# One planned issue order for everything ahead of the query phase of a gated mix of an S4 convolution and Hedgehog linear attention

## The chip, the core and the metric

The kernel runs on one core of a Trainium2 chip. Its engines are PE (matmul), DVE (vector), ACT (activations and casts), POOL and SP (which issues most DMAs). Each engine works through its own list of instructions in order, and waits where an instruction's inputs or its output buffer are not ready. The metric is the time of one execution on the device in microseconds (us); smaller is better.

## What is computed

```python
x = A_u                                            # 1 x 2048 x 512, bf16
g = sigmoid((x * gate_w).sum(-1, keepdims=True))
return g * A(x) + (1 - g) * B(x)

def A(u):      # S4: a kernel K per channel from 128 complex modes, then an FFT convolution of length 2*L
    dt = exp(log_dt)[:, None]
    P = exp((dt * (A_re + 1j*A_im))[:, :, None] * arange(L))
    K = einsum("dn,dnl,dn->dl", C, P, dt * B).real
    return irfft(rfft(u, 2*L) * rfft(K, 2*L))[:L] + u * Dskip

def B(x):      # linear attention, 32 heads of 16, feature map from two softmaxes
    q, k, v = split(x @ wqkv)
    phi(t) = concat(softmax(t @ w_phi), softmax(-(t @ w_phi)))
    kv = einsum("bhsf,bhsd->bhfd", phi(k), v);  z = phi(k).sum(s)
    return ((phi(q) @ kv) / (phi(q) @ z + 1e-6)) @ wo
```

## The kernel before

The program has these stages, in the order of the code in `full_kernel`:

- *Tables* (`build_fft_consts`): sine and cosine tables W1, TB, TI, TJ for an FFT that is done as matmuls. Each comes from an iota (POOL), two DVE instructions and one sine (ACT).
- *Rates* (`compute_rates`): the modes' rates as bf16 pairs, sent through DRAM (`pz`) into `stat`.
- *Polar form* (`compute_polar`): the modes' amplitudes and phases as tables Ctab and Dtab. A long chain between DVE and ACT: products, logarithms, exponentials, an arctangent, then four rounds (`trig4`) of fill, reduction, absolute value, two sines and table products.
- *Data turn* (`turn_x`): x (tile UD) is transposed on PE into xT; eight evictions from PSUM.
- *Projections* (`fold_projection`, twice): w_phi is folded into the key and query weights, Wkp and Wqp.
- *Spectrum* (`u_path`): the FFT of x in two halves; each half is eight psA tiles (evicted into XAu), then eight psB tiles (evicted into XU).
- *Gates* (`gates`): the gate g, and its logarithmic form zrow.
- *Key steps* (`key_step`, eight): pk and vp matmuls (projections of keys and values), exponentials Ek (ACT), their sums Zk (a DVE reduction), reciprocals through Ln and Exp (ACT), vr (DVE scaling of the values), and kvp (PE accumulates all steps in one PSUM bank). The first block's query exponentials Eq and the first decay tables (E, cs) are put between steps 4 and 6.
- *Fold* (`fold_kv`): kvp becomes the weights Mw. Its first instruction is zj, its first ACT instruction the cast KVT.
- *Query phase*: four blocks of 512 rows, with the first kernel generators (`kgen`).
- *Convolution* (`convolve`): the rest of the kernel spectrum, the product and the inverse transform.

Up to the query phase the order on each engine is what the tile framework's scheduler makes of this code. The convolution is issued in another way: `Plan` holds pieces of work, each with an engine, a cost in us, dependencies and the rings of buffers that it takes and drops. `Plan.run` lists the pieces by a greedy rule, the piece that can start first, and of those the one with the longest chain behind it (`prio`), and issues them in that order under `manual_schedule`. `late` is the part of a transfer's cost in which SP is already free.

An activation needs its table set on ACT: TRIG has the sine and arctangent, LN_EXP the logarithm and exponential. Changing the set is an ACT_TABLE_LOAD. Ahead of the query phase there are six: TRIG for the tables, LN_EXP for the rates, TRIG for the polar form's second part, LN_EXP for gates and keys, then TRIG and LN_EXP around the first cosines and sines. Evictions go to ACT and DVE in a fixed pattern (`Evict`, "aav": two of three to ACT).

PSUM has two rings of two double banks ahead of the key steps (tags pb and p0). From then on p0's place holds psA: three single banks (bk) and the accumulator kvp.

Of the kernel before, what the change touches and what calls it, by code (L numbers as in the profile page):

```python
# [83 lines left out]
class Tables:  # L84
# [5 lines left out]
    def begin(self, name):  # L90
        p = self.nc.scalar.preload_act_table_set(name)  # L91
        if self.plain:
            return
        order_after(self.tc, p, self.cur)
        self.head, self.cur = p, [p]

    def __call__(self, **kw):
        i = self.nc.scalar.activation(**kw)  # L98
        if self.plain:
            return i  # L100
        order_after(self.tc, i, self.head)
        self.cur.append(i)
        return i
# [12 lines left out]
class Plan:  # L116
# [4 lines left out]
    def __init__(self, rings):  # L121
        self.k, self.nodes = rings, []

    def add(self, eng, cost, fn, deps=(), take=(), drop=(), late=0.0):
        n = Bag()
        n.eng, n.cost, n.fn, n.take, n.drop, n.late = eng, cost, fn, list(take), list(drop), late
        n.deps = [d for d in deps if d is not None]
        n.users, n.t, n.i = [], None, len(self.nodes)
        for d in n.deps:
            d.users.append(n)  # L130
        self.nodes.append(n)
        return n

    def run(self):

        for r, k in self.k.items():
            if r == "ps":
                continue
# [7 lines left out]
        for n in reversed(self.nodes):  # L146
            n.prio = n.cost + n.late + max([u.prio + self.LAT * (u.eng != n.eng) for u in n.users], default=0.0)
# [5 lines left out]
        while left:  # L153
            best = None
            for n in left:
                if any(d.t is None for d in n.deps):
                    continue
                t = free.get(n.eng, 0.0)
                for d in n.deps:
                    t = max(t, d.end + (self.LAT if d.eng != n.eng else 0.0))  # L160
                ok = True
                for r in n.take:
                    if r != "ps":
# [10 lines left out]
                if best is None or key < best[0]:  # L174
                    best = (key, n)
            assert best is not None, "no piece can start"
            (t, _, _), n = best
            n.t, n.end = t, t + n.cost
            free[n.eng] = n.end - (n.late if n.eng == "SP" else 0.0)
            if "ps" in n.take:  # L180
                n.ps = taken["ps"]
                taken["ps"] += 1
            if "ps" in n.drop:
                given["ps"][[d for d in n.deps if "ps" in d.take][0].ps] = n.end
# [361 lines left out]
def attention_consts(nc, wp, icol, ident, gw, Dcol_b, wc):  # L546
    at = Bag()
# [201 lines left out]

def convolve(tc, nc, g):  # L750

    fc, act, XU = g.fc, g.act, g.XU
    P = Plan({"ps": 4, "E": 4, "cs": 4, "A": 2, "R": 2, "KD": 1, "XA": 2, "XK": 2, "tt": 2, "Z": 1, "Zr": 2, "XUs": 1, "bS": 2})
# [8 lines left out]

    def tables(h, prev):

        T = Bag()
        T.E, T.cs, T.nE, T.nc = [None] * 2, [None] * 2, [], []
        for i in range(2):
            G = 2 * h + i
            for b2 in range(2):
                box = Bag()  # L770

                def pe(i=i, G=G, b2=b2, box=box):
                    if b2 == 0:
                        T.E[i] = g.epool.tile([128, 32, 64], BF16, name="E", bufs=4)
                    box.ps = psum([128, 16, 64], "args")
                    for j in range(2):
                        d0 = 16 * b2 + 8 * j
                        nc.tensor.matmul(box.ps[:, 8 * j:8 * j + 8, :], lhsT=g.stat[0:64, G, :], rhs=g.selE[0:64, d0:d0 + 8, :],  # L778
                                         start=True, stop=True, tile_position=(0, 0))

                def ex(i=i, b2=b2, box=box):
                    act(out=T.E[i][:, 16 * b2:16 * b2 + 16, :], in_=box.ps[:], func=ACT.Exp)
                    box.ps = None
                a = P.add("PE", 0.75, pe, [T.first] if b2 else [], take=["ps"] + (["E"] if b2 == 0 else []))
                T.first = a
                T.nE.append(P.add("ACT", 1.03, ex, [a] + prev, drop=["ps"]))
        b = P.add("ACT", 1.28, lambda: act.begin(TRIG), T.nE)
        for i in range(2):
            G = 2 * h + i
            box = Bag()  # L790

            def pe(i=i, G=G, box=box):
                T.cs[i] = g.epool.tile([128, 2, 32, 32], BF16, name="cs", bufs=4)
                box.ps = psum([128, 32, 32], "args")
                for j in range(2):
                    nc.tensor.matmul(box.ps[:, 16 * j:16 * j + 16, :], lhsT=g.stat[64:128, G, :], rhs=g.selE[64:128, 16 * j:16 * j + 16, 32:64],
                                     start=True, stop=True, tile_position=(64, 0))

            def sc(i=i, box=box):
                act(out=T.cs[i][:, 0], in_=box.ps[:], func=ACT.Sin, scale=TWO_PI, bias=HALF_PI)  # L800
                act(out=T.cs[i][:, 1], in_=box.ps[:], func=ACT.Sin, scale=TWO_PI)
                box.ps = None
            a = P.add("PE", 0.75, pe, [T.nE[2 * i]], take=["ps", "cs"])
            T.nc.append(P.add("ACT", 2.06, sc, [a, b], drop=["ps"]))
        T.end = P.add("ACT", 1.28, lambda: act.begin(LN_EXP), T.nc)
        return T
# [252 lines left out]
    T = {}  # L1059
# [10 lines left out]
    for h in range(2, 8):  # L1070
        if h + 1 < 8:
            T[h + 1] = tables(h + 1, prev)
# [17 lines left out]
def full_kernel(tc, A_u, A_A_re, A_A_im, A_B_re, A_B_im, A_C_re, A_C_im, A_log_dt, A_Dskip,  # L1090
# [7 lines left out]
    with ExitStack() as ctx:  # L1098
# [13 lines left out]
        kpool = pool(ck, "kpool")  # L1112
        cu = ExitStack()
        ps0 = pool(cu, "ps0", 2, space=PSUM)
        ring = PsumRing((psP, "pb"), (ps0, "p0"))
        up = pool(cu, "up", side="right")
        xau = pool(cu, "xau", side="right")
        cp = ExitStack()
        tp = pool(cp, "ctmp", side="right")

        UD = up.tile([128, 64, 128], BF16, name="UD")
        for dj in range(4):
            nc.sync.dma_start(out=UD[32 * dj:32 * dj + 32, :, :], in_=x2d[:, 128 * dj:128 * dj + 128].rearrange("(q t) d -> q t d", t=64))
        rawd = {}
        ldc = up.tile([128, 4], BF16, name="ldc")
        ld_b = up.tile([128, 512], BF16, name="ld")
        gw = aq.tile([128, 4], BF16, name="gw")
        Dcol_b = aq.tile([128, 4], BF16, name="Dcol_b")
        wc = up.tile([128, 4, 16], BF16, name="wc")
        with nc.allow_non_contiguous_dma(reason="small"):  # L1130
            for k, src in (("Are", A_A_re), ("Aim", A_A_im), ("Cre", A_C_re), ("Bre", A_B_re), ("Cim", A_C_im), ("Bim", A_B_im)):
                rawd[k] = up.tile([128, 4, 128], BF16, name=k)
                nc.scalar.dma_start(out=rawd[k][:], in_=src.rearrange("(g p) n -> p g n", p=128))
                if k == "Aim":
                    nc.sync.dma_start(out=ldc[:], in_=A_log_dt.rearrange("(g p) -> p g", p=128))
                    nc.sync.dma_start(out=ld_b[:], in_=A_log_dt.partition_broadcast(128))
            nc.sync.dma_start(out=wc[:], in_=B_w_phi.rearrange("(m h) e f -> (h e) m f", h=8))
            nc.sync.dma_start(out=gw[:], in_=gate_w.rearrange("(kt p) -> p kt", p=128))
# [174 lines left out]
```

## Time and profile before

| | |
|---|---|
| median of 3 runs | 377.31 us (377.28 to 377.91) |
| the profiled execution | 376.3 us, its span 374.5 us |
| mean granted TensorE clock in it | 0.852 |
| busy time | DVE 281.4, PE 266.0, ACT 254.8, POOL 8.6 us |
| instructions | 10448 |

Times below are those of the profiled execution, from the span's start, unless the text says otherwise. A row of the timeline has the start, the busy time, engine, line, operation, output<-inputs, size and count; in square brackets stands the idle time ahead of it and what ended it. A row of the groups has the busy time and the mean of one in ns, and behind the second bar the idle time ahead of them. A matmul's busy time contains its latency, so a busy PE is not PE at its peak.

### The profile page before, as it was taken

Reading aid. Unit: us, or ns where it says so; the run is one execution under the profiler, and the core shown is the slowest. Engines: PE = TensorE matmul, PEld = TensorE weight load, DVE = VectorE, ACT = ScalarE, POOL = GpSimd, SP = SyncE. Lnnn points to the kernel's source line nnn. Section 1 sums busy time; section 2 is a strip of 40 time slices with the busy share of each in tenths; the row PEclk is TensorE's granted clock in tenths of the full one; section 3 lists DMA queues with packets and bytes.
Section 4 is the critical chain, followed back from the end, with each engine's and each line's share of the span. In section 5 each row is a group of like instructions: output and inputs, shape, how many; then the busy total and the mean of one; then the engine's idle time right before and its main releaser. Section 6 shows DMA issues by size and latency. Waiting matters only on the chain. (4 is left out here: it accounts for less than half of the span.)

```text
span 374.5 us, 10448 instructions
## 1 busy us (share of the span) xinstructions
PE 266.0 (71%) x4632; PEld 156.6 (42%) x4632; DVE 281.4 (75%) x481; ACT 254.8 (68%) x329; POOL 8.6 (2%) x21
## 2 busy tenths in 40 slices
PE   1225465858997769889998799766778558669662
PEld 0115365755343323334454355333334324437561
DVE  6979778886587537779994545999999997879122
ACT  1668979885744872688647852797799975895520
POOL 4400000000000000000000000000000000000000
PEclk9999996667899966999999999958589856685967
DMA  9994000000000000000000010553957782875311
GB/s 153 161 242 107 0 0 3 2 2 2 0 2 3 2 0 2 2 3 30 28 30 30 8 51 30 137 118 103 162 77 125 158 168 63 147 152 100 61 32 32
DMA packets 77948, 23.62 MB, mean 63 GB/s; under 512 B 72656, under 2 KB 75856, under 8 KB 77904
## 3 DMA queue, kind: packets, MB, share of 16 engines
q1 hardware_dynamic: 73680, 22.05, 29.6%
q10 hardware_dynamic: 4224, 0.92, 1.8%
q8 instruction: 36, 0.59, 0.7%
q14 instruction: 8, 0.07, 0.1%
HBM read 10.90 MB, written 7.86 MB: 50 GB/s over the span
## 5 line engine op out<-in xcount | busy, mean ns | idle before, releaser
L98 ACT ACTIVATE E<-args 128x1024 bf16<-128x1024 f32 x32 | 31.9, 1039 | 4.9 <-PE args L395 4.5
L742 PE MATMUL bps<-Mw,Eq 128*128 128x512 bf16 x128 | 30.4, 380 | 2.5 <-DVE Eq L738 2.3
L645 DVE TENSOR_REDUCE Zk<-Ek 128x64 f32<-128x1024 bf16 x16 | 19.2, 1214 | 17.1 <-ACT Ek L98 17.1
L98 ACT ACTIVATE cs<-args 128x1024 bf16<-128x1024 f32 x32 | 30.9, 1047 | 0.0
L91 ACT ACT_TABLE_LOAD x20 | 25.7, 1283 | 5.4 <-issue 5.1
L738 DVE TENSOR_TENSOR Eq<-Eq,aexp 128x512 bf16<-128x512 bf16 x32 | 20.5, 681 | 11.3 <-PE aexp L735 11.2
L98 ACT ACTIVATE Ek<-pk 128x512 bf16<-128x512 f32 x32 | 17.4, 602 | 13.5 <-PE pk L642 13.5
L450 PE MATMUL kps<-R,A 128*32 128x64 bf16 x1024 | 21.3, 235 | 4.8 <-DVE R L844 4.1
L450 PEld LDWEIGHTS <-A 128*32 128x32 bf16 x1024 | 18.6, 152 | 13.4 <-issue 10.5
L1213 ACT CAST bs<-bps 128x512 bf16<-128x512 f32 x16 | 9.4, 586 | 21.5 <-PE bps L745 17.0
L657 DVE TENSOR_TENSOR vr<-vp,vr 128x512 bf16<-128x512 f32 x32 | 19.9, 682 | 5.3 <-ACT vr L98 4.6
L932 ACT CAST XK<-psB 128x1024 bf16<-128x1024 f32 x16 | 15.9, 1029 | 9.8 <-PE psB L924 8.3
L959 PE MATMUL psz<-t,TI 128*128 128x512 bf16 x48 | 17.0, 477 | 7.3 <-DVE t L939 3.0
L642 PE MATMUL pk<-Wkp,xT 128*128 128x512 bf16 x64 | 20.6, 437 | 1.8 <-ACT Ek L98 1.8
L655 PE MATMUL vp<-Wv,xT 128*128 128x512 bf16 x64 | 19.1, 425 | 2.9 <-ACT Ek L98 2.9
L476 PE MATMUL psB<-XAu,TB 64*128 64x128 bf16 x256 | 12.6, 280 | 11.1 <-ACT XAu L70 4.4
L98 ACT ACTIVATE Eq<-pq 128x512 bf16<-128x512 f32 x32 | 16.5, 612 | 4.2 <-PE pq L699 4.0
L591 PE MATMUL xps<-ident,UD 128*128 128x128 bf16 x64 | 7.5, 311 | 15.7 <-ACT bim L305 9.2
L778 PE MATMUL args<-selE,stat 64*128 64x512 bf16 x40 | 14.6, 476 | 5.4 <-ACT cs L98 2.8
L742 PEld LDWEIGHTS <-Eq 128*128 128x128 bf16 x128 | 11.3, 98 | 16.3 <-DVE Eq L738 4.3
L924 PE MATMUL psB<-XA,TB 64*128 64x64 bf16 (+1 forms) x640 | 12.0, 192 | 7.4 <-issue 1.9
L830 DVE TENSOR_TENSOR A<-A,Atmp 128x1024 bf16<-128x1024 bf16 x24 | 16.6, 692 | 0.8
(228 smaller groups left out, 624.7 us busy)
## 6 DMA issues: line engine op xcount, KB each, us to landing
XUs<-XU SPq DMA_DIRECT2D x6, 512.0 KB, 6.0
Zd<-Zr SPq DMA_DIRECT2D x12, 256.0 KB, 2.2
ZT<-Zd SPq DMA_DIRECT2D x24, 128.0 KB, 3.9
UD<-in_A_u_dram SPq DMA_DIRECT2D x4, 512.0 KB, 11.3
bSd<-bs SPq DMA_DIRECT2D x16, 128.0 KB, 1.7
out_dram<-bS SPq DMA_DIRECT2D x30, 64.0 KB, 2.6
bS<-bSd SPq DMA_DIRECT2D x3, 512.0 KB, 6.1
wqk<-in_B_wqkv_dram SPq DMA_DIRECT2D x1, 1024.0 KB, 5.8
```

The lines of the kernel that those rows point to most:

```text
L91: p = self.nc.scalar.preload_act_table_set(name)
L98: i = self.nc.scalar.activation(**kw)
L450: nc.tensor.matmul(kps[32 * dj:32 * dj + 32, g4, e, :], lhsT=A[:, ri, :, :, d].rearrange("p a b -> p (a b)"), rhs=R[:, ri, d, :], start=(r ...
L642: nc.tensor.matmul(pk[:], lhsT=xT[:, kt, ss], rhs=Wkp[:, kt, :], start=(kt == 0), stop=(kt == 3))
L645: nc.vector.tensor_reduce(out=Zk[:, u, :, :], in_=Ek[:, u, :, :].rearrange("p g (h f) -> p g h f", f=16), axis=mybir.AxisListType.X, op=AL ...
L655: nc.tensor.matmul(vp[:], lhsT=xT[:, kt, ss], rhs=Wv[:, kt, :], start=(kt == 0), stop=(kt == 3))
L657: nc.vector.tensor_tensor(out=vr[:, u, sg, :, 0:32].rearrange("p m (h e) -> p m h e", e=16), in0=vp[:].rearrange("p (m h e) -> p m h e", m ...
L738: nc.vector.tensor_tensor(out=e, in0=e, in1=ps[:], op=ALU.mult)
L742: nc.tensor.matmul(ps[:], lhsT=Eq[:, m, sg, 128 * i:128 * i + 128], rhs=Mw[:, 4 * sg + m, :], start=(k == 0), stop=False, skip_group_check ...
L830: nc.vector.tensor_tensor(out=c.A[:, o], in0=c.A[:, o], in1=tmp[:], op=op)
L932: nc.scalar.copy(out=box.XK[:].rearrange("p s (c e x) -> p (s c) e x", e=2, x=16), in_=box.ps[:].rearrange("p e s (c x) -> p (s c) e x", x ...
L959: nc.tensor.matmul(box.ps[:, 4 * hb:4 * hb + 4, :], lhsT=fc.TI[:, k].rearrange("p a b -> p (a b)"), rhs=box.t[k][:, rt:rt + 4, :], start=( ...
```

## The change

The stages from the tables to the last key step, with the first Eq block and the first tables E and cs, become pieces of one `Plan` (`prepare` and `keys_and_spectrum`), which is issued by hand order, as the convolution already is. The arithmetic stays as it was. What else changes:

- A piece can name keys that it reads and writes (`rw`), from which its dependencies follow. Several PSUM rings can be given out in the order of the plan (`dyn`).
- An eviction can go to ACT or DVE; the plan takes the engine on which it ends first, at costs of 1.1 and 1.3.
- Temporary tiles of the tables and of the polar form get fixed places (`tgv`, `pt`, `pb`, names in the rows below) instead of a ring of nine.
- The transfers start in another order: SP loads log_dt ahead of the four UD loads, and ACT loads its first table set ahead of issuing the six parameter loads.
- The key steps' order allows two steps at a time (Ek, Zk and vr have two buffers, as before).
- `prio` is now `cost` plus the longest chain behind, without adding `late` a second time. This reorders the convolution too.

In the core of the diff, `box`, eviction and load functions are left out:

```diff
-    def add(self, eng, cost, fn, deps=(), take=(), drop=(), late=0.0):
+    def add(self, eng, cost, fn, deps=(), take=(), drop=(), late=0.0, rw=("", "")):
...
+        for k in rw[0].split() + rw[1].split():
+            wr, rd = self.keys.setdefault(k, (None, []))
+            n.deps += ([wr] if wr is not None else []) + (rd if k in rw[1].split() else [])
...
-            n.prio = n.cost + n.late + max([u.prio + self.LAT * (u.eng != n.eng) for u in n.users], default=0.0)
+            n.prio = n.cost + max([u.prio + self.LAT * (u.eng != n.eng) for u in n.users], default=0.0)
...
+def prepare(P, tc, nc, g, evict, psum0):
...
+    t1 = S(1.3, lambda: act.begin(TRIG), w="act")
...
+    S(2.6, params, w="raw0", deps=[t1])
+    P.add("SP", 4.0, lambda: g.load_ld(), late=3.0, rw=("", "ldc ldb"))
+    P.add("SP", 8.0, lambda: None, late=7.9, rw=("raw0", "raw"))
+    for dj in range(4):
+        P.add("SP", 4.0, lambda dj=dj: g.load_ud(dj), rw=("", f"ud{dj}"))
+    P.add("SP", 4.0, lambda: g.load_w(), late=2.0, rw=("", "wsm wqk"))
...
+def keys_and_spectrum(tc, nc, g):
...
+    P = Plan({"XAu": 1, "Ek": 2, "Zk": 2, "vr": 2, "E": 4, "cs": 4}, {"ps": 2, "bk": 3, "p0": 2})
...
+        n.p = P.add([("ACT", 1.1), ("DVE", 1.3)], 1.2, f, deps, drop=[ring])
+        return n.p
+    polar, xt, kp, at_n = prepare(P, tc, nc, g, evict, psum0)
+    lnexp = P.add("ACT", 1.3, lambda: act.begin(LN_EXP), [polar])
...
+            a = P.add("PE", 1.3, pa, [a] if g4 else last, take=[ring] + (["XAu"] if g4 == 0 else []), rw=("ud0 ud1 ud2 ud3 W1", ""))
+            en.append(evict(ea, [a], ring))
...
+            a = P.add("PE", 1.4, pb, en + [a], take=[ring], rw=("TB0 TB1 TB2", ""), drop=(["XAu"] if r0 == 28 else []))
...
+    a = P.add("PE", 4.0, ga, xt + [at_n], take=["ps"])
...
+    a = P.add("PE", 2.0, gd, [b, sp], take=["ps"])
+    P.add("DVE", 0.6, ge, [a], drop=["ps"])
...
+            a = P.add("PE", 1.2, pk, [a] if u else [sp, lnexp] + xt + kp, take=["bk"] + ([] if u else ["Ek", "Zk", "vr"]))
+            x = P.add("ACT", 1.22, ex, [a] + ([x] if u else []), drop=["bk"])
+            red.append(P.add("DVE", 1.21, rd, [x] + red))
...
+        l = P.add("ACT", 0.6, ln, red, drop=["Zk"])
...
+            a = P.add("PE", 1.2, pv, [a], take=["bk"], rw=("wqk", ""))
+            c = P.add("DVE", 1.36, sc, [a, l], drop=["bk"])
+            kv = [P.add("PE", 0.9, kn, [c] + kv, drop=(["Ek", "vr"] if u else []))]
...
+        a = P.add("PE", 1.2, pq, [sh, sp] + ([a] if m else []), take=["bk"])
+        b = P.add("ACT", 1.22, qe, [a], drop=["bk"])
+    sl = P.add("DVE", 3.0, lambda: g.selectors(), [sh, sp, g.n_stat])
+    T = plan_tables(P, nc, g, psum, 0, [n for n in P.nodes if n.eng == "ACT"], [sl])
+    with tc.manual_schedule():
+        act.plain = True
+        P.run()
+        act.plain = False
+    return Q.e, (T.E, T.cs)
```

Three places show how instructions move. The first is on ACT, around its second table load (LN_EXP, ahead of the rates). `tj`, `TI`, `TB` and `w` are parts of the FFT tables. Before:

```order
L98 ACTIVATE w_162<-tg_v,mpi 128x32 x2
L98 ACTIVATE TB<-tg_v,mpi 128x32x64 x2
L98 ACTIVATE TI<-tg_v,mpi 128x64 x2
L98 ACTIVATE tj<-tg_v,mpi 128x1024 x2
L91 ACT_TABLE_LOAD
L98 ACTIVATE dtc<-ldc 128x4
L98 ACTIVATE dt<-ld 128x512
```

and after:

```order
L99 ACTIVATE TB<-tgv_155,mpi 128x32x64
L99 ACTIVATE tj<-tgv_154,mpi 128x1024
L99 ACTIVATE tj<-tgv_155,mpi 128x1024
L1101 CAST XAu<-psA 128x256x4
L91 ACT_TABLE_LOAD
L99 ACTIVATE dtc<-ldc 128x4
L922 COPY pt_261<-psri 128x512
```

A cast of the spectrum's first half, which needs UD, now stands ahead of the load and so ahead of dtc, the first instruction of the rates.

The second place is on ACT around its fourth table load (LN_EXP for the keys). `trg` is a sine of the polar form. Before:

```order
L98 ACTIVATE trg<-big_n 128x1024
L70 CAST XU<-psB 128x32x32 x2
L91 ACT_TABLE_LOAD
L70 CAST XU<-psB 128x32x32 x4
L70 CAST wT_1013<-wtp 128x1024
L70 CAST Wqp<-wps 128x1024
L98 ACTIVATE E<-args 128x1024
L98 ACTIVATE gz<-gz 128x16
L98 ACTIVATE E<-args 128x1024
L98 ACTIVATE Ek<-pk 128x512 x5
```

and after:

```order
L99 ACTIVATE trg<-pb_266 128x1024
L1101 CAST xT<-xps 128x8x4x32 x2
L91 ACT_TABLE_LOAD
L1101 CAST XAu<-psA 128x256x4
L99 ACTIVATE Ek<-pk 128x512 x8
L99 ACTIVATE Zk<-Zk 128x128
L99 ACTIVATE vr<-Zk 128x64x2
L1101 CAST XU<-psB 128x32x32
L99 ACTIVATE Ek<-pk 128x512 x6
```

The key steps come right behind the last XAu cast, and the second half's XU casts, the query projection (wT, Wqp), gate (gz) and tables (E) stand among or behind the key steps.

The third place is on DVE at the start of the key steps. Before:

```order
L259 TENSOR_TENSOR selE<-m_1167,b_1171 128x2048
L68 CAST Wqp<-wps 128x1024
L620 TENSOR_SCALAR gz<-gps 128x16
L631 TENSOR_SCALAR zrow<-zps 128x512
L622 TENSOR_SCALAR gz<-gz 128x16
L623 RECIPROCAL gT<-gz 128x16
L645 TENSOR_REDUCE Zk<-Ek 128x64 x3
L657 TENSOR_TENSOR vr<-vp,vr 128x16x32 x4
L645 TENSOR_REDUCE Zk<-Ek 128x64
```

and after:

```order
L924 TENSOR_TENSOR Dtab<-Dtab,trg 128x4x256 x3
L1099 CAST XAu<-psA 128x256x4 x2
L1258 TENSOR_REDUCE Zk<-Ek 128x64 x4
L1282 TENSOR_TENSOR vr<-vp,vr 128x16x32 x8
L1258 TENSOR_REDUCE Zk<-Ek 128x64 x3
L1099 CAST XU<-psB 128x32x32
L1258 TENSOR_REDUCE Zk<-Ek 128x64
```

The reductions and scalings of two steps stand together, four and eight, and selectors, gate and zrow have left the place ahead of them.

More of the change, by code (lines that the diff above doesn't have):

```diff
@@ L761, in convolve @@
     rkn, xan = [0], [0]
[L763 to L806, printed above, removed]
     def kgen(h, T, XA, new):
@@ L1112, in full_kernel @@
         kpool = pool(ck, "kpool")
+        cz = ExitStack()
         cu = ExitStack()
[L1114 to L1117, printed above, removed]
         cp = ExitStack()
[L1119 to L1123, printed above, removed]
@@ L1130, in full_kernel @@
[L1130 to L1138, printed above, removed]
-            nc.sync.dma_start(out=Dcol_b[:], in_=A_Dskip.rearrange("(kt p) -> p kt", p=128))
@@ new lines, in shift_tmp, with free_tmp, shift_psum @@
+        def shift_tmp():
+            cp.close()
+            g.ctmp = None
+            g.ptmp = pool(cp, "ptmp", side="right")
+        def free_tmp():
+            cp.close()
+            g.kwk = pool(ck, "kwk", 2)
+            g.wo = g.kwk.tile([128, 4, 512], BF16, name="wo_sb", bufs=1)
+            nc.sync.dma_start(out=g.wo[:], in_=B_wo.rearrange("(kt p) c -> p kt c", p=128))
+        def shift_psum():
+            cz.close()
+            g.psA = pool(ca, "psA", 3, space=PSUM)
+            g.kvp = g.psA.tile([128, 8, 34], F32, name="kvp", tag="acc", bufs=1)
```

643 lines of the change are left out of this document (568 added, 75 removed).

## The prediction

> **What bounds the kernel now.** I read the page's busy line first, then the busy time by stages, then the chain, then the timeline at the seams between stages.
>
> ```profile
> PE 266.0 (71%) x4632; PEld 156.6 (42%) x4632; DVE 281.4 (75%) x481; ACT 254.8 (68%) x329; POOL 8.6 (2%) x21
> ```
>
> No engine is full over the whole span, so the question goes to the stages. The columns are the stretch, then busy us of PE, PEld, DVE, ACT and POOL, the granted TensorE clock, the DMA share and GB/s.
>
> ```profile
> 20.00:43.00 23.00, 9.49 (x80) 8.40 (x79) 19.36 (x39) 18.79 (x29) 0.00 (x0) 1.00 0.48 138
> 43.00:77.00 34.00, 22.13 (x272) 19.89 (x272) 28.41 (x45) 27.89 (x30) 0.18 (x1) 0.78 0.00 1
> 77.00:96.00 19.00, 15.50 (x249) 10.92 (x250) 12.46 (x18) 13.85 (x16) 0.00 (x0) 0.68 0.01 2
> 96.00:129.00 33.00, 28.41 (x360) 12.24 (x359) 22.09 (x27) 19.83 (x41) 0.00 (x0) 1.00 0.01 2
> 129.00:147.00 18.00, 13.22 (x156) 4.56 (x156) 10.32 (x14) 11.05 (x18) 0.00 (x0) 0.63 0.00 1
> 147.00:156.60 9.60, 8.35 (x156) 3.69 (x155) 6.23 (x9) 4.24 (x9) 0.00 (x0) 0.98 0.01 2
> 156.60:234.00 77.40, 70.00 (x781) 36.26 (x780) 56.21 (x108) 51.29 (x80) 0.00 (x0) 1.00 0.08 25
> 234.00:346.00 112.00, 80.62 (x1765) 45.47 (x1766) 103.41 (x167) 92.29 (x96) 0.00 (x0) 0.74 0.64 126
> ```
>
> From 43 to 96 ACT and DVE share the polar form and the evictions. From 96 to 156.6 the key steps run: PE is at 50.0 us of 60.6, DVE at 38.6, ACT at 35.1. The first stretch is limited by ACT and DVE, the second by PE and by the round trip between engines, and they stand one behind the other. The query phase (156.6 to 234, PE 90%) and the convolution (DVE 92%) follow and do the same work after the change. The change touches what lies before 156.6, plus the order of the convolution. The seams:
>
> ```profile
> 19.77 0.11 PEld L591 LDWEIGHTS <-UD 128*128 128x128 bf16 x1 [5.53 <-issue]
> 20.72 1.28 ACT L91 ACT_TABLE_LOAD   x1
> 42.91 0.63 ACT L98 ACTIVATE cbi<-cbi 128x512 f32<-128x512 f32 x1
> 81.91 1.28 ACT L91 ACT_TABLE_LOAD   x1
> 95.92 2.20 ACT L98 ACTIVATE Ek<-pk 128x512 bf16<-128x512 f32 x4 [0.58 <-PE pk L642]
> 156.58 0.17 DVE L672 TENSOR_TENSOR zj<-kvp,mask 128x16 f32<-128x16 f32 x1 [0.65 <-PE kvp L663]
> 159.26 1.01 ACT L686 CAST KVT<-ktp 128x1024 bf16<-128x1024 f32 x1
> ```
>
> Here 19.77 is when the matmul side first gets UD, 42.91 is the arctangent (the last step of the polar chain before its trig part), 95.92 the first key exponential, 156.58 the start of the fold. Each term below is a shift of one of these.
>
> **The change, part by part.** The amounts of work stay: PE has the same count of matmuls, ACT the same table loads. Only places move.
>
> *Front, to the arctangent.* SP issues the small log_dt loads ahead of the four UD loads.
>
> ```profile
> 0.73 11.81 SPq L1123 DMA_DIRECT2D UD<-in_A_u_dram  x4
> 12.59 3.22 SPq L1135 DMA_DIRECT2D ldc<-in_A_log_dt_dram  x1
> ```
>
> UD then starts 1 to 4 us later (two short issues, or the whole 3.22 and more), and lands at about 21 to 24. In the new order ACT has one XAu cast, which needs UD, ahead of its second table load: the load moves from 20.72 to about 23 to 25, and the rate and polar chain with it. Against that, ACT evicts less between that load and the arctangent: before it has four xT casts there, now two XAu casts, worth 2 x 1.0 us (DVE has four casts there instead of three). ACT's first table load goes ahead of its six parameter loads; the parameters start 1.28 us later and are needed only behind the second load, so that is hidden, as long as UD, not they, lands last. I take 0 for the arctangent, bounds -1 and +3.
>
> *From the arctangent to the first key step.* This is the main term. Before, 53.0 us lie between 42.91 and 95.92; in them stand the rest of the polar form, both halves of the spectrum, both projections, gates, selectors and two tables. In the new order the key steps' first exponentials come right behind ACT's fourth table load (back to LN_EXP) and one XAu cast. What stands before them on ACT from the arctangent on: 20 casts, 12 polar activations, the arctangent and one load. The eight casts of the spectrum's second half, the second projection, selectors, gates and tables have gone behind. Their prices:
>
> ```profile
> L70 ACT CAST XAu<-psA 128x1024 bf16<-128x1024 f32 x11 | 10.6, 1021 | 2.3 <-PE psA L463 2.2
> L98 ACT ACTIVATE trg<-big_a 128x1024 bf16<-128x1024 f32 x4 | 4.2, 1044 | 0.0
> L98 ACT ACTIVATE Ek<-pk 128x512 bf16<-128x512 f32 x32 | 17.4, 602 | 13.5 <-PE pk L642 13.5
> L645 DVE TENSOR_REDUCE Zk<-Ek 128x64 f32<-128x1024 bf16 x16 | 19.2, 1214 | 17.1 <-ACT Ek L98 17.1
> L657 DVE TENSOR_TENSOR vr<-vp,vr 128x512 bf16<-128x512 f32 x32 | 19.9, 682 | 5.3 <-ACT vr L98 4.6 <-PE vp L655 0.7
> ```
>
> Busy per cast is 10.6 / 11 = 0.96 us (the mean of 1.02 overlaps its neighbour). So 20 x 0.96 + 12 x 1.04 + 0.63 + 1.28 = 33.6 us without a wait. DVE's list over the same stretch comes to about the same: nine casts, the four fills with their reductions, and the table products. ACT was busy 82% of 43 to 77; I take 92%, between that and full, because two kinds of work can now fill each other's waits: 36.5 us, to 79.4, and about 0.5 for the last pk. First key exponential at 79.9 instead of 95.9: **-16.0**. Bounds: no waits, -19; the old 82%, 83.9 + 0.5, -11.5.
>
> *The key steps.* They take 60.7 us now (95.92 to 156.58). The order now does them two at a time: four reductions, then eight scalings on DVE (4 x 1.2 + 8 x 0.62 = 9.8 us), and PE loads vp for both before kvp. Four such pairs are 39 us of DVE. Into the gaps go what was moved behind: eight spectrum casts (7 on ACT, 1 on DVE), four projection casts, selectors 2.7, and the tables.
>
> The price of that is on PE. Its work here at full clock:
>
> ```profile
> 96.83 1.89 PE L655 MATMUL vp<-Wv,xT 128*128 128x512 bf16 x8
> 132.07 1.89 PE L655 MATMUL vp<-Wv,xT 128*128 128x512 bf16 x4
> L476 PE MATMUL psB<-XAu,TB 64*128 64x128 bf16 x128 | 6.0, 277 | 4.0 <-ACT big_n L360 3.4 <-ACT XU L70 0.7
> L618 PE MATMUL gps<-gw,xT 128*128 128x1 bf16 x64 | 1.8, 165 | 0.0
> L627 PE MATMUL zps<-xT,gwr 128*32 128x512 bf16 x16 | 1.9, 628 | 0.0
> ```
>
> Eight matmuls at clock 1.00 cost what four cost in the slow stretch. Counting 129 to 147 at 0.63, PE's 50.0 us are 45 at full clock. The change brings psB 6.0, the second projection about 2.3, gps 1.8, zps 1.9: 12 more, so 57. PE's best share over a long stretch is 70.0 of 77.4, 0.90: 57 / 0.90 = 63.3 us. DVE gives a like figure: 39 + 5.7 for the moved work + about 2.5 of restart after each of three pairs + 6 at the end, where vp waits for the tables' exponentials and the last kvp stand behind zps, which needs a bank that the sines give back: 59. I take 63.5: **+2.8**. Bounds 57 and, with the clock as in 129 to 147, 57 / 0.63 = 90.
>
> The clock decides here: stretches with PE at 86 to 90% show 0.98 to 1.00, those at 65 to 82% show 0.63 to 0.78. The new stretch would have 90%. The Trainium skill ("TensorE: Matmul & The Clock Gate", Part 1) says that the clock is halved by default and that about 3.4 us of sustained matmuls release it; these rows agree. By that rule alone the sum would take the 59 us of the DVE count rather than 63.5.
>
> *Fold to query phase.* ACT has a table load and six Eq exponentials ahead of KVT, whose input is ready 2.7 us after the fold starts (159.26 - 156.58). 1.28 + 6 x 0.54 = 4.5, partly during the last kvp: **+1.5**, bounds 0 and +3.
>
> *The convolution's order.* The planner no longer adds a transfer's late part twice when it ranks pieces, so the rows from 234 on stand differently. At the end:
>
> ```profile
> 346.43 1.31 PE psz L993 x66
> 349.31 0.99 PE psz L993 x38
> 350.30 0.98 PE psA L874 x8
> 351.71 0.62 PE psy L1035 x69
> 359.93 4.29 PE psz L993 x151
> ```
>
> psA stood behind both psz groups and psB behind psy; now psA follows the first psz group, and psB precedes psy. That is worth up to 3 us of the last chain. In the middle DVE has 112.0 - 103.4 = 8.6 us of idle, which another order may halve or double, and nothing here shows which: **-2**, bounds -6 and +6.
>
> Sum: 0 - 16.0 + 2.8 + 1.5 - 2 = -13.7. The profiled execution took 376.3 (span 374.5 and 1.8 around it), so 362.6; the median of the runs, 377.3, is 1.0 above it. I say 363.
>
> **Rivals.** *Fuller overlap.* ACT and DVE run 43 to 79 without waits (-19), PE keeps clock 1.00 and the key steps take 59 (-1.7), the convolution gives 4: about 352 to 354. For it: the query phase reaches 90% on PE. Against: the order's engines are strict queues, and its prices for PE (1.2 for a pk that takes 1.03) shift the real waits.
>
> *The waits move.* The two-at-a-time order waits on banks: vp 4 of a pair cannot start until DVE frees one of three. With the old 82% (-11.5), key steps of 68 (+7.3) and the convolution at 0: 376.3 - 11.5 + 7.3 + 1.5, 373.6; by half of that, 369. For it: ACT idles 13.5 before Ek on pk, and DVE 17.1 before Zk, in the group rows above.
>
> *The clock stays low in the key steps: slower.* PE then carries 57 us of work at about 0.63, as from 129 to 147: 90 us, +29.8 instead of +2.8: 376.3 + 13.3, about 390. It decides where the key steps take 60.7 + 16.0 - 1.5 + 2 = 77 us, a mean clock of 0.74. For it: 43 to 77 and 129 to 147 had PE gaps at every bank change, and the new order puts such changes into the key steps. Against: PE had these at 96 to 129 too and kept 1.00. The Trainium skill ("TensorE: Matmul & The Clock Gate", A second HAM failure mode) describes just that: cycling through PSUM banks leaves small idles, and the clock swings.
>
> *Nothing gained.* Term 2 could fail if the key steps have no room for what is moved; then the fold starts where it did, and the result is within 1 us. The 9.6 us that PE idles in 96 to 156.6 speak a little for it, since 12 us come in.
>
> **How the numbers follow.** Forecast (357 to 369): 0.58. Fuller overlap (below 357): 0.18. Waits move (369 to 376.5): 0.14. Nothing gained: 0.03. Clock low or another new stall (above 378): 0.07. The range 352 to 373 leaves out the slower cases and the outermost of the others, about 2 in 10. A measurement of this kernel cannot tell less than about 0.2%, 0.75 us, from no change; faster 0.90, same 0.03, slower 0.07.
>
> **What would show it.** The arctangent at 42 to 46; ACT's fourth table load near 76 to 81 and the first Ek within 2 us behind the last XAu cast; zj at 141 to 147; PE busy near 90% and clock near 1.0 in the key steps; KVT 3 to 5 us behind zj; the query phase 77 us as now; from the end of the query phase to the end of the span 138 to 143 us, against 140.5. It would be wrong if UD landed after 26, if the clock were below 0.75 from 80 to 145, or if the convolution lost more than 6.

## The result, and the profile after

The changed kernel took 368.88 us (median; 365.77 to 370.0), the kernel before beside it 377.61 us: ratio 0.975, 95% interval 0.970 to 0.980. Forecast were 363.0 us, with a range of 352 to 373. The profiled execution took 365.77 us (span 364.0), the shortest of its runs; the sum below is made against it. Medians are of all executions, ratios and their intervals of the undisturbed ones alone, and since load_first, front_free and ldc_ahead were profiled in a disturbed execution, only the front is read from their traces.

The busy line of the page after, and then the busy time by the prediction's seams: the first five rows are of the kernel before (arctangent, first Ek, zj, KVT, last bs cast, end), the second five the same seams after. The columns are those of the prediction's table of stretches.

```profile
PE 257.8 (71%) x4594; PEld 151.6 (42%) x4632; DVE 283.0 (78%) x480; ACT 254.5 (70%) x330; POOL 12.4 (3%) x24
```

```profile
42.91:95.92 53.01, 37.55 (x521) 30.81 (x522) 40.92 (x62) 41.75 (x46) 0.18 (x1) 0.75 0.01 1
95.92:156.58 60.66, 50.05 (x670) 20.50 (x669) 38.62 (x49) 35.18 (x67) 0.00 (x0) 0.88 0.01 1
156.58:159.26 2.68, 2.18 (x19) 1.05 (x21) 2.59 (x12) 2.59 (x6) 0.00 (x0) 1.00 0.00 0
159.26:235.90 76.64, 69.74 (x779) 36.28 (x776) 55.50 (x101) 49.15 (x76) 0.00 (x0) 1.00 0.08 27
235.90:374.50 138.60, 93.68 (x2547) 57.20 (x2545) 107.80 (x171) 99.28 (x102) 0.00 (x0) 0.75 0.57 109
```

```profile
47.53:83.43 35.90, 24.82 (x291) 20.15 (x291) 33.20 (x51) 32.13 (x35) 0.29 (x2) 0.69 0.00 1
83.43:138.76 55.33, 49.67 (x898) 25.61 (x908) 44.20 (x57) 43.43 (x77) 0.00 (x0) 1.00 0.01 2
138.76:142.80 4.04, 3.41 (x35) 1.76 (x37) 3.00 (x14) 4.03 (x7) 0.00 (x0) 1.00 0.02 4
142.80:223.20 80.40, 71.87 (x762) 36.87 (x761) 55.06 (x97) 49.88 (x77) 0.00 (x0) 0.96 0.08 26
223.20:364.00 140.80, 96.35 (x2534) 58.07 (x2545) 108.25 (x171) 99.33 (x102) 0.00 (x0) 0.73 0.55 108
```

| stretch | before | after | measured | predicted |
|---|---|---|---|---|
| start to arctangent | 42.9 | 47.5 | +4.6 | 0 |
| arctangent to first key exponential | 53.0 | 35.9 | -17.1 | -16.0 |
| key steps, to zj | 60.7 | 55.3 | -5.3 | +2.8 |
| zj to KVT | 2.7 | 4.0 | +1.4 | +1.5 |
| KVT to the last bs cast (query phase) | 76.6 | 80.4 | +3.8 | 0 |
| last bs cast to the end (convolution) | 138.6 | 140.8 | +2.2 | -2 |
| sum | | | -10.4 | -13.7 |

The first stretch after the arctangent holds the largest fall, and both less work and less idle time: ACT is busy for 32.1 of 35.9 us and DVE for 33.2, where each was busy for about 41 of 53. The seams themselves, from the timelines of SP, DVE and ACT after:

```profile
1.78 16.48 SPq L1728 DMA_DIRECT2D UD<-in_A_u_dram  x4
25.61 0.69 DVE L571 TENSOR_TENSOR Wphi<-wc,mask 128x512 bf16<-128x512 bf16 x1 [3.63 <-DMA wc<-in_B_w_phi_dram]
26.64 1.01 ACT L1101 CAST XAu<-psA 128x1024 bf16<-128x1024 f32 x1 [5.39 <-PE psA L1122]
27.66 1.28 ACT L91 ACT_TABLE_LOAD   x1
47.53 0.63 ACT L99 ACTIVATE pt<-pt 128x512 f32<-128x512 f32 x1
79.23 1.28 ACT L91 ACT_TABLE_LOAD   x1
81.61 1.01 ACT L1101 CAST XAu<-psA 128x1024 bf16<-128x1024 f32 x1 [1.09 <-PE psA L1122]
83.43 3.04 ACT L99 ACTIVATE Ek<-pk 128x512 bf16<-128x512 f32 x6 [0.81 <-PE pk L1246]
138.76 0.17 DVE L688 TENSOR_TENSOR zj<-kvp,mask 128x16 f32<-128x16 f32 x1
142.80 1.07 ACT L702 CAST KVT<-ktp 128x1024 bf16<-128x1024 f32 x1
```

ACT stands for 5.39 us at an XAu cast that needs UD, and its second table load comes 6.9 us later than before (27.66, was 20.72). DVE stands at Wphi for wc, which is issued behind UD. The table load at 79.23 and the first Ek 1.8 us behind the start of the last XAu cast are where the prediction had them.

### The profile page after: what moved, and what is told of

It is laid out like the page before. It is cut to its first block, busy times and chain, and to the rows that moved or that the text cites. A ratio compares the mean times of both kernels' runs of the same rounds, so it can differ in the third digit from the quotient of the medians.

```text
span 364.0 us, 10417 instructions
## 1 busy us (share of the span) xinstructions
PE 257.8 (71%) x4594; PEld 151.6 (42%) x4632; DVE 283.0 (78%) x480; ACT 254.5 (70%) x330; POOL 12.4 (3%) x24
## 5 line engine op out<-in xcount | busy, mean ns | idle before, releaser
L758 PE MATMUL bps<-Mw,Eq 128*128 128x512 bf16 x119 | 32.0, 405 | 3.5 <-DVE Eq L754 2.8
L1122 PE MATMUL psA<-W,UD 128*64 128x256 bf16 x128 | 15.6, 404 | 16.8 <-DMA UD<-in_A_u_dram 9.2
L1537 PE MATMUL psz<-t,TI 128*128 128x512 bf16 x38 | 18.2, 542 | 11.4 <-DVE t L1517 6.9
L1122 PEld LDWEIGHTS <-UD 128*64 128x64 bf16 x128 | 12.0, 205 | 19.2 <-issue 15.8
L1517 DVE TENSOR_TENSOR t<-XU,XK 128x1024 bf16<-128x1024 bf16 x16 | 11.0, 688 | 10.7 <-ACT XK L1510 10.7
L1342 PE MATMUL args<-selE,stat 64*128 64x512 bf16 x48 | 15.8, 442 | 4.8 <-ACT cs L99 2.8
L1421 DVE TENSOR_TENSOR R<-E,cs 128x1024 bf16<-128x1024 bf16 x24 | 16.5, 686 | 1.6 <-ACT cs L99 1.6
L1278 PE MATMUL vp<-Wv,xT 128*128 128x512 bf16 x62 | 15.4, 381 | 3.0 <-DVE vr L1282 2.8
```

The costliest lines, as they stand in the source:

```text
L758: nc.tensor.matmul(ps[:], lhsT=Eq[:, m, sg, 128 * i:128 * i + 128], rhs=Mw[:, 4 * sg + m, :], start=(k == 0), stop=False, skip_group_check ...
L1122: nc.tensor.matmul(box.ps[64 * e:64 * e + 64, i, :], lhsT=g.UD[:].rearrange("p t (e g) -> p g e t", e=2)[:, gw * h + 4 * g4 + i, e, :], rh ...
L1421: nc.vector.tensor_tensor(out=c.R[:, o, :, 32:64], in0=E[:, :, 32:64], in1=x, op=ALU.mult)
L1537: nc.tensor.matmul(box.ps[:, 4 * hb:4 * hb + 4, :], lhsT=fc.TI[:, k].rearrange("p a b -> p (a b)"), rhs=box.t[k][:, rt:rt + 4, :], start=( ...
```

## The experiments

The theory after the result: the front's 4.6 us come from UD landing late; the convolution's new order costs about 2 us; and the 3.8 us of the query phase are a stretch of low TensorE clock that is not tied to a place in the program. Rivals: the front is slow from the order of ACT and DVE; the 2.2 us are one execution's clock; the query phase loses by its order. Medians, and ratios with their 95% intervals:

| kernel | median us | ratio to before, 95% |
|---|---|---|
| after_again | 367.75 | 0.9753 (0.9701 to 0.9804) |
| ud_first | 358.53 | 0.9521 (0.9477 to 0.9566) |
| load_first | 366.35 | 0.9646 (0.9588 to 0.9703) |
| conv_late | 365.46 | 0.9716 (0.9677 to 0.9755) |
| before_nolate | 376.77 | 1.0016 (0.9990 to 1.0042) |
| keys_last | 375.56 | 0.9973 (0.9947 to 1.0000) |
| both | 356.72 | 0.9503 (0.9455 to 0.9551) |
| front_free | 360.96 | 0.9506 (0.9454 to 0.9558) |
| ld_ahead | 364.14 (2 runs) | 0.9641 (0.9466 to 0.9815) |

ldc_ahead has two runs, 366.26 and 360.30 us, and no ratio. From the traces come the seams, and the time that the granted clock stood at half between the first Ek and the last bs cast, read in slices of 0.4 us:

| trace | arctangent at | first Ek to last bs | of it at half clock | last bs to end |
|---|---|---|---|---|
| before | 42.9 | 140.0 | 13.6 | 138.6 |
| after | 47.5 | 139.8 | 6.8 | 140.8 |
| after_again | 47.1 | 141.5 | 12.3 | 141.5 |
| ud_first | 42.5 | 137.4 | 1.2 | 139.9 |
| conv_late | 47.0 | 140.8 | 11.8 | 139.4 |
| before_nolate | 43.7 | 139.7 | 11.0 | 141.5 |
| keys_last | 47.0 | 135.8 | 13.6 | 141.5 |
| both | 42.5 | 137.4 | 1.4 | 139.4 |
| ld_ahead | 46.4 | 137.4 | 1.1 | 140.9 |

**after_again: the same kernel, a second trace.**

> The changed kernel once more, unaltered, as the measure for the other runs and for a second trace. Its first runs took 365.8 to 370.0 us, and the profiled one was the fastest of them. Theory: from the first key exponential to the last bs cast it takes 140 us as before (139.8 in the first trace, 140.0 before the change), with one stretch at a low TensorE clock in it, some 10 to 18 us long, whose place may change: the key steps then take 55 us and the query phase 80, or the key steps 59 to 61 and the query phase 76 to 77. Rival: the query phase always pays 4 us more than before (80 to 81 us from KVT to the last bs cast) and the key steps always take 55, because of what the new order does and not because of the clock. Time by either: 366 to 370.

It took 367.75 us. From the first Ek to the last bs cast lie 141.5 us, and the low stretch has moved: in the first trace it lay at 196, here at 149.6, behind the fold. The key steps took 55.9 us and the query phase 81.5, as the rival said, so this pair of traces alone does not part theory from rival; the third trace with the same order on PE, ACT and DVE (ud_first) does. Its rows stand below those of after_again; each pair is the same piece of the program, 8.6 us of the fold and the 10 us behind it:

```profile
141.00:149.60 8.60, 6.15 (x73) 2.92 (x73) 4.77 (x14) 7.89 (x14) 0.00 (x0) 1.00 0.01 2
149.60:159.80 10.20, 9.67 (x68) 3.51 (x68) 6.92 (x13) 7.30 (x9) 0.00 (x0) 0.52 0.00 1
```

```profile
136.40:145.00 8.60, 6.30 (x73) 2.92 (x73) 4.77 (x14) 7.89 (x14) 0.00 (x0) 1.00 0.01 2
145.00:155.00 10.00, 8.82 (x93) 4.38 (x94) 9.76 (x19) 9.96 (x13) 0.00 (x0) 1.00 0.04 14
```

In the first 8.6 us all engines do the same, DVE and ACT to the hundredth. Then one execution falls to half clock for 10.2 us, and the other does not. With a low stretch in it the query phase takes 80.4 and 81.5 us, without one 77.6 (ud_first), 77.5 (both) and 77.6 (ld_ahead). Before the change it took 76.6 at clock 1.00. So its order costs 1 us, and the rest is the clock. The 140 us that the theory took for the whole stretch are not fixed either: without a low stretch behind the start of the key steps it is 137.4.

**ud_first: UD ahead of the log_dt loads on SP.**

```diff
-    P.add("SP", 4.0, lambda: g.load_ld(), late=3.0, rw=("", "ldc ldb"))
+    P.add("SP", 4.0, lambda: [g.load_ud(dj) for dj in range(4)], late=3.0, rw=("", "ldc ldb"))
-        P.add("SP", 4.0, lambda dj=dj: g.load_ud(dj), rw=("", f"ud{dj}"))
+        P.add("SP", 4.0, lambda dj=dj: g.load_ld() if dj == 3 else None, rw=("", f"ud{dj}"))
```

> Only SP's order is changed: the four UD loads are issued ahead of the two log_dt loads again, as before the change; every other engine keeps the new order. Theory (the front's 4.6 us come from UD, and with it wc, landing 5.7 us later): UD lands near 20, the first XAu cast stands at 21 to 22, ACT's second table load at 22 to 23 instead of 27.7, the arctangent at 42.5 to 44 instead of 47.5, and the time falls by 3.5 to 5 us against the changed kernel run beside it. Rival (the front is bound by the order of DVE and ACT, with tables made later and the bitwise-and steps slowed beside POOL): the arctangent stays behind 46 and the time falls by less than 1.5 us.

```profile
0.73 12.22 SPq L1728 DMA_DIRECT2D UD<-in_A_u_dram  x4
21.43 1.01 ACT L1101 CAST XAu<-psA 128x1024 bf16<-128x1024 f32 x1 [0.17 <-PE psA L1122]
22.46 1.28 ACT L91 ACT_TABLE_LOAD   x1
42.51 0.63 ACT L99 ACTIVATE pt<-pt 128x512 f32<-128x512 f32 x1
```

The arctangent stands at 42.51, 0.4 us earlier than before the change, so the whole front term came from the place of the log_dt loads ahead of UD. The time fell by 9.2 us against after_again, more than the 3.5 to 5 expected: 4.6 in the front, 4.1 between the first Ek and the last bs cast (all but 1.2 us of it at full clock in this trace), 1.6 behind it. Its six runs took 356.4 to 365.6 us.

**load_first: ACT's second table load ahead of the first XAu cast.** The eviction of psA also depends on the load: `en.append(evict(ea, [a, P.gate], ring))`.

> The first XAu casts may stand only behind ACT's second table load, so that this load needn't wait for UD; SP's order stays new. Theory: the table load moves from 27.7 to about 21.5, but DVE still stands at Wphi until wc lands at 25.6 and has 2.5 us of attention constants behind it, so the rate chain starts near 28.3 instead of 29.2: arctangent 46 to 47.5, time 0 to -1.5 us against the changed kernel. Rival (the table load's wait for UD is by itself what delays the front): arctangent at 42 to 43, time -4 to -5 us.

```profile
21.28 1.28 ACT L91 ACT_TABLE_LOAD   x1
25.39 0.69 DVE L571 TENSOR_TENSOR Wphi<-wc,mask 128x512 bf16<-128x512 bf16 x1 [3.40 <-DMA wc<-in_B_w_phi_dram]
27.68 0.69 DVE L886 SCALAR_TENSOR_TENSOR pt<-Are,dtc 128x512 f32<-128x512 bf16 x1
46.02 0.63 ACT L99 ACTIVATE pt<-pt 128x512 f32<-128x512 f32 x1
```

Against after_again the load moved by 6.0 us (from 27.24) and the arctangent by 1.1 (from 47.12): DVE stands at wc, as the theory said. Two engines wait for the same late queue, and freeing one of them moves the front by 1.1 us. The medians differ by 1.4 us; the ratios differ by more (0.9646 against 0.9753), with intervals that just meet, and no row of the front accounts for that.

**ldc_ahead and ld_ahead: which small load holds UD up.** One of the two is issued ahead of UD, the other behind it.

```diff
+    P.add("SP", 4.0, lambda: [g.load_ld(0), g.load_ud(0)], late=3.0, rw=("", "ldc ldb"))
+        P.add("SP", 4.0, lambda dj=dj: g.load_ud(dj + 1) if dj < 3 else g.load_ld(1), rw=("", f"ud{dj}"))
```

> Which of the two small loads ahead of UD holds it up? In the changed kernel only ldc (512 pieces of 2 bytes) is issued ahead of the four UD loads, ld (128 rows of 1 KB) behind them. Theory (the small pieces of ldc take the queue's time): the first XAu cast stays at 25 to 26.5, as with both ahead, against 21.4 with UD first. Rival (ld costs it, or each costs its issue time alone): the first XAu cast at 22 to 23.5. Time by the front: within 1 us of the changed kernel, or 3 us less.

> The other half: ld alone is issued ahead of UD, ldc behind it. Theory: the first XAu cast at 21.5 to 23, near the kernel with UD first. Rival (ld, or any load ahead of UD, costs the 5 us): 25 to 26.5.

First with ldc ahead, then with ld ahead: the first XAu cast, and a row of windows from 6 to 14 us, with its length and then the granted clock, the DMA share and the GB/s of all the core's transfers. The last row is that window with UD first.

```profile
23.29 1.01 ACT L1101 CAST XAu<-psA 128x1024 bf16<-128x1024 f32 x1 [2.03 <-PE psA L1122]
6.00:14.00 8.00, 1.00 1.39 161
```

```profile
25.47 1.01 ACT L1101 CAST XAu<-psA 128x1024 bf16<-128x1024 f32 x1 [4.21 <-PE psA L1122]
6.00:14.00 8.00, 1.00 1.39 148
```

```profile
6.00:14.00 8.00, 1.00 1.40 171
```

The theory falls in both, and the rival with ld as the cause holds. Against 21.43, ldc costs 1.9 us and ld 4.0; both together 4.8 to 5.2 (26.22 and 26.64). The first matmuls on UD give the same differences: they start at 20.27 with UD first, then at 22.13, 24.31, and at 25.06 and 25.48 with both ahead. The dear one is ld, 128 copies of one row of 1 KB, though SP issues it in 0.4 to 0.5 us: behind it the transfers move 148 GB/s instead of 171. Why a broadcast row slows what comes behind it isn't shown. The Trainium skill ("DMA: Bandwidth & Descriptors", Rules for kernel authors) says that a last dimension that isn't contiguous is moved as one descriptor for each element; by that rule ldc is 512 descriptors, which is why the theory took it for the dear one; the runs charge it less than half of what they charge ld.

**keys_last: the overlap undone.** The plan lets the key steps start only behind the whole spectrum and the second projection (`a.hold = [] if u else u0 + last`, where `hold` counts for the time and not for `prio`); everything up to ACT's fourth table load stays.

> The changed kernel, but in the plan the key steps may start only when the whole spectrum and the second projection are done; the order up to ACT's fourth table load stays. This undoes the overlap and leaves the rest. Theory (the key steps take in 12 us of PE work that fitted beside them, and 4 to 8 us of the gain is this overlap): first key exponential at 96 to 100 instead of 83, the key steps 47 to 51 us instead of 55 to 56, KVT 6 to 9 us later, time 373 to 377. Rival 1 (the key steps are bound by their round trips and the moved work costs them nothing): key steps still 55 us, time +12 to +15, 380 or more. Rival 2 (the moved work costs the key steps as much as it takes by itself): KVT within 2 us, time within 2 us of the changed kernel.

```profile
46.98:96.33 49.35, 33.60 (x533) 27.96 (x532) 36.11 (x58) 43.61 (x48) 0.00 (x0) 0.78 0.01 1
96.33:143.42 47.09, 40.56 (x665) 18.28 (x664) 38.88 (x50) 29.80 (x63) 0.00 (x0) 1.00 0.01 2
143.42:148.49 5.07, 4.21 (x68) 2.24 (x66) 3.00 (x14) 5.04 (x6) 0.00 (x0) 1.00 0.01 3
```

First Ek 13.3 us later than in after_again, key steps 8.8 us shorter, fold 1.0 longer: KVT 5.5 us later (148.49 against 142.96), the time 7.8 us longer by the medians. So the overlap is worth 5.5 us at KVT. The time agrees with the theory (373 to 377), KVT falls half a us short of it (6 to 9). The larger surprise is the middle row: without the moved work the key steps take 47.1 us, where they took 60.7 before. They run two at a time, at clock 1.00 and not 0.88, and hold less PE work. The groups of PE in the key steps, keys_last first, then before:

```profile
L1292 PE MATMUL kvp<-vr,Ek 128*32 128x34 bf16 x512 | 6.2, 181 | 1.3 <-DVE vr L1283 1.1
L1310 PE MATMUL pq<-xT,Wqp 128*128 128x512 bf16 x16 | 4.0, 380 | 0.0
```

```profile
L663 PE MATMUL kvp<-vr,Ek 128*32 128x34 bf16 x512 | 8.8, 183 | 5.8 <-DVE vr L657 5.8
L699 PE MATMUL pq<-xT,Wqp 128*128 128x512 bf16 x26 | 7.3, 382 | 0.0
```

Some of the query projections pq stand behind zj now, and kvp, which waited 5.8 us for DVE's vr in short pieces, runs with 1.3 us of waits. Part of that wait has gone to vp, which waits 4.9 us for vr in keys_last (2.9 us, for Ek, before). In all, PE's idle time in the key steps fell from 10.6 to 6.5 us and its busy time from 50.0 to 40.6.

**conv_late, before_nolate, both: the convolution's order.** conv_late counts `late` twice again for the convolution's plan alone (`n.cost + self.twice * n.late + max(...)`, with `P.twice = 1` in `convolve`); before_nolate takes it out of the kernel before; both is conv_late with ud_first.

> The planner adds the transfers' late part twice again, for the convolution's plan alone; up to the query phase everything stays new, and the convolution's order is that of before on each engine. Theory (the new convolution order is the slower one by the 2.2 us seen in the first trace): from the last bs cast to the end of the span 138 us instead of 140.2, time -1.5 to -3 us against the changed kernel. Rival (the 2.2 us are the clock of one execution): within 1 us of it. Second rival (the new order gains, as was predicted): +1 to +3 us.

> The kernel before, with one part of the change alone: the planner no longer adds the transfers' late part twice, which gives the convolution the changed kernel's order on every engine; all that stands ahead of it is as before. Theory (this order costs 1.5 to 2.5 us): from the last bs cast to the end of the span 140 to 141.5 us instead of 138.6, time +1.5 to +2.5 us against before, ratio 1.004 to 1.007. Rival (the difference was the clock of single executions): ratio within 0.002 of 1. Predicted before the change was run: -2 us.

> UD first on SP and the convolution's order of before, in the changed kernel. If the two add up: the arctangent at 42.5, from the last bs cast to the end 138 to 139.5 us, and 1.5 to 2.5 us less than with UD first alone: 355.5 to 357.5 us as a median. If the convolution's order gained only by the clock of its executions: 358 to 359.

From the last bs cast to the end the new order took 140.8, 141.5, 139.9, 141.5, 141.5 and 140.9 us in six traces, the old one 138.6, 139.4 and 139.4 in three: 141.0 against 139.1, and the two sets don't meet. The times only lean the same way: -2.3 us for conv_late against after_again, -1.8 for both against ud_first, +0.2 for before_nolate against before, with an interval of -0.1% to +0.4% that holds no change. In before_nolate the time came out as its rival said (within 0.002 of 1), though its seam stands where the theory put it (141.5), and its interval ends at 1.6 us. So the seam shows about 2 us, in single traces; the times show less, and do not tell it from nothing where this order alone was changed. The chain of before_nolate, in shares of the span, names a candidate:

```profile
by line: PE psz L993 3.1%; issue 1.6%; DMA ZT<-Zd 1.4%; DMA Zd<-Zr 1.2%; ACT cs L98 0.9%; PE psy L1035 0.7%; DVE bS L1044 0.6%; ACT Zr L965 0.5%; PE psB L924 0.5%; PE psy L1023 0.5%; ACT XA L880 0.4%; DVE t L939 0.4%; ACT L91 0.3%; DVE Z L1
```

The last turn through DRAM (Zd, then ZT) is on it, as in every trace of the new order, and isn't on the chain of before. But conv_late and both have the old order and ZT on their chains too, so this is a candidate only, not shown. The kernel called both is the fastest here: 356.72 us, 0.9503.

**front_free: both, and the rate chain let go.** As both, with load_first's dependency, and DVE's attention constants behind the statistics.

> As the kernel with both changes, and besides ACT's second table load stands ahead of the first XAu cast, and DVE's attention constants may stand only behind the statistics that it hands to the DMA. With UD first the constants held the rate chain until 24.2 while dtc was ready at 23.9. Theory: the table load at 21.3, the rate chain from 22.8, the arctangent at 40.5 to 41.5 instead of 42.5, 1 to 2 us less than the kernel with both changes. Rival: the XAu cast that the plan now puts on DVE ahead of the rate chain waits for UD, and the arctangent stays at 42 to 42.5: no change.

```profile
21.27 1.28 ACT L91 ACT_TABLE_LOAD   x1
21.63 1.22 DVE L1100 CAST XAu<-psA 128x1024 bf16<-128x1024 f32 x1
22.80 0.69 DVE L887 SCALAR_TENSOR_TENSOR pt<-Are,dtc 128x512 f32<-128x512 bf16 x1
42.96 0.63 ACT L99 ACTIVATE pt<-pt 128x512 f32<-128x512 f32 x1
```

The rate chain starts at 22.80 instead of 24.18 (both), and the arctangent still stands at 42.96. The rival's outcome came, no change, and not by its reason: the XAu cast on DVE waits for nothing there. The gain is given back later, where the plan put the attention constants and two more XAu casts of ACT between rate chain and arctangent. The ratio, 0.9506, is that of both (0.9503).

## Why the prediction was right, and where its steps failed

The direction, the main term and the range were right; the 363.0 us were 5.9 too low against the median, 2.8 against the profiled execution. The median lies at the upper end of the stretch that the prediction called its forecast (357 to 369). That it came so near is in part luck: four of the six stretches were off by 3.8 to 8.1 us, three of them upward and one downward.

- *Front, "I take 0 for the arctangent, bounds -1 and +3": failed.* It priced the two small loads ahead of UD at 1 to 4 us; it was about 5.7 (the XAu tiles' matmuls wait for it until 25.5, the data turn had it at 19.77). It also counted ACT's wait alone: wc and with it DVE's constants came late too. The measured +4.6 lies outside the bounds. With UD first the term is -0.4.
- *Arctangent to first key exponential, -16.0: right.* 35.9 us against 37.0 forecast, and 35.5 to 35.9 in all traces with this order up to the first Ek, at a mean clock of 0.69 (after) as of 0.79 (both). ACT was 90% busy, forecast 92%; DVE, whose list the prediction took to be as long, was 92% busy.
- *Key steps, +2.8: wrong by 8.1 us.* The step is "PE's 50.0 us are 45 at full clock" and the 12 us added to it. At clock 1.00 the steps themselves show 40.6 us of PE (keys_last), since part of pq had left them (it was booked in the fold's term alone) and kvp is tighter; the moved work, read in the groups after (the rows below: spectrum, second projection, gates), is 5.0 + 1.2 + 1.1 + 1.7 + 1.0 = 10.0. That is 50.6 and not 57. PE was 49.67 of 55.33 us busy, 0.90, just the share that was taken. The order of two steps at a time was booked as a cost of the DVE cycle. In keys_last, where the steps run in that order without the spectrum's and the gates' work beside them, they are 13.6 us shorter than before; no run shows how much of that is the pairing. (Two figures of this step do not add up as they stand: the DVE count is 58.2, not 59, and PE's idle time from 96 to 156.6 is 10.6 us, not 9.6. Neither changes the step.)

```profile
L493 PE MATMUL psB<-XAu,TB 64*128 64x128 bf16 x128 | 5.0, 218 | 0.0
L1206 PE MATMUL gps<-gw,xT 128*128 128x1 bf16 x64 | 1.7, 164 | 0.0
L1177 PE MATMUL wps<-Wphi,wT 128*128 128x128 bf16 x16 | 1.2, 220 | 0.0
L1161 PE MATMUL wtp<-ident,wqk 128*128 128x128 bf16 x16 | 1.1, 220 | 0.0
L1225 PE MATMUL zps<-xT,gwr 128*32 128x512 bf16 x16 | 1.0, 381 | 0.2 <-ACT cs L99 0.2
```

- *Where the gain arises.* The prediction booked terms two and three as one move of work beside the key steps. From the arctangent to KVT lie 116.4 us before, 95.9 in after_again, and 101.5 where the overlap is undone (keys_last). So of 20.5 us the overlap gives 5.7, and the other 14.8 come without it: a denser first stretch (49.4 us, was 53.0, with nearly the same work in it) and shorter key steps (47.1, was 60.7, fold 2.4 longer). Part of the 14.8 is clock: the trace before had 13.6 us at half clock in the key steps, that of keys_last none, and in the table each further us of it cost 0.32 to 0.43 us (139.8, 141.5 and 140.8 against 137.4), so an estimate is 5 us for the clock and 10 for the order. A second reading needs no price for the clock: from the arctangent to the last bs cast lie 193.0 us in before, 185.1 in keys_last and 177.4 in after_again, and from the first Ek on these three hold nearly the same time at half clock (13.6, 13.6 and 12.3 us). There 7.9 us come without the overlap and 7.7 by it. Which part of the new order gives the 7.9 (two steps at a time, the placing of the evictions, the fixed places of the tiles) no run shows. By the whole time, the order without the overlap gains next to nothing (ratio 0.9973): against before, the front (+4.1), the query phase (+7.0) and the convolution (+2.9) take it back.
- *Fold, +1.5: right* (+1.4).
- *Query phase, 77 us "as now": the work is right* (77.5 to 77.6 where the clock stays up), the measured 80.4 has 6.8 us at half clock. The rival "the clock stays low in the key steps" did not come. In the two traces of the changed kernel the long low stretches lie in the query phase instead (at 196 and at 149.6); in conv_late, with the same order there, 6.8 us of them lie in the key steps again, which then take 58.7 us, and the query phase 79.2. From the first Ek to the last bs cast the two profiled executions differ by 0.2 us.
- *Clock, "these rows agree": too strong.* The prediction's own table has a row against its rule that PE's share tells the clock: from 20 to 43 PE is 41% busy at clock 1.00. The rows of after_again and ud_first say the same: after 8.6 us with PE busy for 72 and 73%, the clock falls in one and not in the other.
- *Convolution, -2: wrong sign*, +2.2 in the trace, about +2 at the seam over nine traces, less in the times. The step is reading the last chain's rows (psA and psB moved up, "worth up to 3 us") as a gain; bounds of -6 and +6 held it.

By these seams the errors are +4.6 in the front, +4.2 in the convolution and +3.8 in the query phase against -1.1 in the stretch to the first Ek and -8.1 in the key steps: near 363 by errors of opposite sign.

## What to carry to other kernels

Where a plan moves a small load ahead of a large one, price not its issue time but what the large transfer loses behind it, and list every engine that waits for what is queued behind both. Read the work of a stage from a stretch in which the clock stood at 1.00 before adding to it, and set apart the stretches of low clock before saying which stage lost or gained. If two engines wait for the same late queue, freeing one of them shows little of what the queue costs.

## What the hardware showed that was not expected

*In these traces the clock falls for whole multiples of one time.* All low stretches that begin between 88 and 215 us in the nine traces of the table last 3.4, 6.8 or 10.2 us, and the same instructions with the same waits fall in one execution and not in another (the rows of after_again and ud_first). The Trainium skill ("TensorE: Matmul & The Clock Gate", Part 1) describes a free-running window of about 3.4 us in which the activity of PE is judged; these lengths agree. That the place of the window against the program decides is in line with both, but no run set it.

*POOL can stop DVE.* DVE's bitwise step over 2048 columns took 3.10 us after, 1.22 before; the rows are DVE and POOL after, then DVE before:

```profile
4.73 3.10 DVE L829 TENSOR_SCALAR tgv<-tgv 128x2048 int32<-128x2048 int32 x1
```

```profile
4.77 1.99 POOL L35 IOTA tgc<- 128x2048 f32 x1 [1.15 <-DVE tgv L828]
```

```profile
8.60 1.22 DVE L207 TENSOR_SCALAR tg_v<-tg_v 128x2048 int32<-128x2048 int32 x1
```

3.10 is 1.22 and 1.88 more, almost the whole iota of 1.99 that started beside it. The Trainium skill ("SBUF — State Buffer", SBUF: two separate sides) says that VectorE and GpSimd have one shared port pair, which an instruction that uses it holds to its end while the other engine stands still; the lengths agree. The rows do not show why DVE, which began 0.04 us ahead, was the one to wait. Not every DVE step is held: steps of one column beside the iota at 1.13 (1.99 us) took 0.14 to 0.15 us each. In the changed kernel all this is hidden behind UD. In front_free it is not: there ACT stands until 20.11 for the DVE step on TJ, which took 1.25 us beside POOL's memsets and 0.42 before, and the table load comes right behind. What that costs wasn't tried.
